# Channel mixing with seven block products, in an order planned at build time, and with re-arranged loads and stores

## The chip, the cores and the metric

One core of a Trainium2 chip runs the whole kernel. The metric is the device time of one execution in microseconds (us), and the median over executions is quoted. The profile is one execution taken by the hardware profiler; its span is 1 to 3 us shorter than the time of the same run. Engines are named as in the profile: PE is TensorE's matmuls, PEld its weight loads, DVE is VectorE, ACT ScalarE, POOL GpSimd, SP SyncE. Lines such as L807 are lines of the kernel in question. PSUM is the memory into which the matmuls write, used by the changed kernel as eight banks; SBUF holds the kernel's other tiles. A DMA transfer lands when its data have arrived. The granted clock is the share of TensorE's full clock that the profile shows. A run counts as slow when it is over 1.5% above the fastest of the same kernel.

A ratio below is formed from the fast runs of a kernel and of the kernel before in the same rounds, so it is not quite the ratio of the medians that stand beside it.

## The reference

```python
# q, k, v: (8, 8, 1024, 64); E, F: (64, 1024)
k_proj = einsum('ks,bhsd->bhkd', E, k); v_proj = einsum('ks,bhsd->bhkd', F, v)
attn   = softmax(q @ k_proj^T / 8) @ v_proj           # per batch and head
x      = attn as (8, 1024, 512)
u      = x + (relu(x^T @ w_tok1) @ w_tok2)^T          # token mixing
out    = u + relu(u @ w_ch1) @ w_ch2                  # channel mixing, 512 -> 1536 -> 512
```

Channel mixing is the largest part: three quarters of the old kernel's necessary matmul time.

## The kernel before

Batches run in a software pipeline: while channel mixing of batch b runs, the attention and token mixing ("front") of batch b+1 is dealt out between its blocks. The two channel products, for half a batch (512 tokens) at a time:

```python
def ch1(i, cc):                       # 12 times per half batch
    g_ps = psC.tile([P, S2], F32, ...)
    for dc in range(DMC):             # 4 matmuls of 512 columns
        nc.tensor.matmul(g_ps, wc1_sb[:, dc, cc*P:(cc+1)*P], uT[i][:, :, dc, :], ...)
    nc.scalar.activation(out=st["gT", i][:, cc, :], in_=g_ps, func=ACT.Relu)

def ch2(i, ss, part):                 # 4 rows x 3 parts per half batch
    for cc in range(part*4, part*4 + 4):
        nc.tensor.matmul(o2_ps, st["gT", i][:, cc, ss*P:(ss+1)*P], wc2_sb[:, cc, :], ...)
    if part == CC // 4 - 1:
        nc.vector.tensor_add(out=o_sb, in0=o2_ps, in1=u_sb[:, si, :])
        nc.sync.dma_start(out=out_v[b, :, si, :], in_=o_sb)
# ... (cut)
def q_transpose():                    # q of batches 1 to 7, by DMA, in SyncE's queue
    nc.sync.dma_start_transpose(out=qT[...], in_=q_sb[...])
```

The transposes of u (also DMA) and the stores of the output share SyncE's queue. Loads of k, v, q are double-buffered and issued from GpSimd's queue.

The softmax here doesn't subtract the row's maximum and nothing guards it: scores larger than these inputs give would overflow.

## Time and profile before

| what | value | where it is read |
|---|---|---|
| time | 502.83 us median of 3 (502.06 to 507.38) | timing runs |
| PE busy, whole span | 91% | page, part 1 |
| first channel product | 41.97 us | timeline of PE |
| stalls | mostly between 60 and 127 us | page, part 2; chain of waits |
| one batch in the steady state | 54.6 us | the same line returning in the chain |
| last matmul to the end | 3.9 us | timeline |

Part 1 of the page of the kernel before (busy us, share of the span, instructions), and rows of its part 2 (the span in 40 slices, tenths busy; PEclk is the granted TensorE clock):

```profile
PE 455.1 (91%) x2556; PEld 221.8 (44%) x2592; DVE 165.6 (33%) x304; ACT 167.3 (33%) x275; POOL 48.9 (10%) x72
...
PE   2689945975899999999999999999999999999996
...
PEclk9999995997899999999999999999999999999999
DMA  8999999999599249855592249505020411123102
```

From the twelfth slice on PE is 90% busy or more. In slices 6, 7, 9 and 10 it is 40 to 79% busy while the DMA engines are full, and the granted clock falls in slices 7, 10 and 11. The same in a table by windows (columns: window, its length, busy us of PE, PEld, DVE, ACT, POOL, granted clock, DMA share, GB/s):

```profile
60.00:80.00 20.00, 8.53 (x58) 3.26 (x55) 2.23 (x4) 6.72 (x12) 0.00 (x0) 0.83 1.22 192
...
150.00:200.00 50.00, 49.52 (x267) 23.46 (x271) 17.94 (x33) 19.06 (x32) 4.44 (x6) 1.00 0.64 132
```

The chain of the work that ended last, in order of time (start us, us, what):

```profile
51.68 29.44 DMA qT<-q_sb
...
106.90 20.44 DMA uT_698<-u_sb
...
173.85 1.73 PE o_ps L364 x8
...
228.43 1.73 PE o_ps L364 x8
...
283.01 1.73 PE o_ps L364 x8
```

Two DMA transposes take 29 and 20 us from issue to landing here, beside the loads; the median of q's transposes is 5.0 us, and those of u from 173 us on take 3.6 to 3.9. After them the chain is PE, and one of its lines comes back every 54.6 us. Two lines of PE's timeline say how fast matmuls go when nothing holds them back (start us, us until the last one ends, what, how many):

```profile
44.57 0.39 PE L286 MATMUL ut_ps<-ident,u_sb 128*128 128x128 bf16 x4
44.80 0.67 PE L276 MATMUL up_ps<-hT_sb,wt_sb 128*128 128x128 bf16 x8
```

From 44.57 to 44.80 PE starts four matmuls of 128 columns, each with its own weights: about 57 ns each. Matmuls of 512 columns start every 0.216 us. So in this trace the time follows the columns at these two sizes, and loading weights, a new set for every matmul, does not bind at either.

### The profile page before, as it was taken

What the parts mean: (1) busy time and instruction counts of PE and PEld (TensorE: products, weight loads), DVE (VectorE), ACT (ScalarE), POOL (GpSimd) and SP (SyncE); (2) the same over time, 40 slices, a digit from 0 to 9 for tenths busy, and PEclk for the clock granted to TensorE, in tenths of its full rate; (3) what the DMA queues carried; (4) which work ended last, traced back from release to release, by engine and by line L of the source; (5) the groups of instructions that cost most, each with busy time, mean ns of one, the idle gap of its engine ahead of it and who ended that gap; (6) DMA issues with size and microseconds to landing.
All of it is one profiled execution on the core that took longest, in us unless ns stands there. A gap on an engine that the chain in (4) does not pass through costs nothing.

```text
span 502.0 us, 6139 instructions
## 1 busy us (share of the span) xinstructions
PE 455.1 (91%) x2556; PEld 221.8 (44%) x2592; DVE 165.6 (33%) x304; ACT 167.3 (33%) x275; POOL 48.9 (10%) x72
## 2 busy tenths in 40 slices
PE   2689945975899999999999999999999999999996
PEld 1457412532345444544444444544444444444442
DVE  2354011533134332614242423533261424241102
ACT  1136641000453316150624135231615053423150
POOL 7533101301201002100200020000000000000000
PEclk9999995997899999999999999999999999999999
DMA  8999999999599249855592249505020411123102
GB/s 124 208 204 206 198 196 180 174 204 219 140 191 196 42 140 149 172 99 137 110 195 63 67 110 189 138 16 153 1 84 1 120 49 42 43 63 106 58 27 84
DMA packets 97211, 61.48 MB, mean 122 GB/s; under 512 B 60320, under 2 KB 88480, under 8 KB 97184
## 3 DMA queue, kind: packets, MB, share of 16 engines
q0 software_dynamic: 29728, 29.63, 36.5%
q1 hardware_dynamic: 67456, 31.46, 25.1%
q8 instruction: 20, 0.33, 0.2%
q14 instruction: 7, 0.06, 0.0%
HBM read 59.24 MB, written 16.78 MB: 151 GB/s over the span
## 4 chain that ended last, share of the span: by engine, by line
PE 73%; DMA 19%; ACT 3%; DVE 2%; POOL 1%; issue 1%; POOLq 0%
PE o_ps L364 31%; PE g_ps L353 26%; DMA qT<-q_sb 6%; PE h_ps L239 5%; PE u_ps L248 4%; DMA uT_698<-u_sb 4%; DMA q_sb<-in_q_dram 4%; DMA wc_sb<-in_moe_w_ch_dram 3%; PE o_ps L221 3%; PE kv_ps L174 2%; DMA v_sb<-in_v_dram 2%; PE s_ps L209 2%; ACT gT L357 1%; DMA out_dram<-o_sb 1%; DVE kp_sb L182 1%
## 5 line engine op out<-in xcount | busy, mean ns | idle before, releaser
L364 PE MATMUL o_ps<-wc_sb,gT 128*128 128x512 bf16 x738 | 183.3, 384 | 1.7 <-issue 0.2
L357 ACT ACTIVATE gT<-g_ps 128x512 bf16<-128x512 f32 x192 | 113.0, 600 | 213.7 <-PE g_ps L353 205.3
L353 PEld LDWEIGHTS <-wc_sb 128*128 128x128 bf16 x768 | 72.6, 98 | 91.8 <-issue 13.8
L364 PEld LDWEIGHTS <-gT 128*128 128x128 bf16 x768 | 73.5, 99 | 80.2 <-issue 4.8
L371 DVE TENSOR_TENSOR o_sb<-o_ps,u_sb 128x512 f32<-128x512 f32 x64 | 44.2, 691 | 90.1 <-PE o_ps L364 83.2
L252 DVE TENSOR_TENSOR u_sb<-u_ps,x_sb 128x512 bf16<-128x512 f32 x56 | 38.6, 690 | 87.7 <-PE u_ps L248 87.7
L214 ACT ACTIVATE a_sb<-s_ps 128x1024 bf16<-128x1024 f32 x32 | 32.1, 1033 | 41.8 <-PE s_ps L209 41.8
L229 DVE TENSOR_TENSOR x_sb<-o_ps,rdn 128x512 bf16<-128x512 f32 x64 | 44.2, 691 | 2.2
L248 PE MATMUL u_ps<-hT_sb,wt_sb 128*128 128x512 bf16 x112 | 34.1, 387 | 6.7 <-DVE u_sb L252 6.7
L228 DVE RECIPROCAL rdn<-o_ps 128x8 f32<-128x8 f32 x64 | 13.1, 204 | 64.8 <-PE o_ps L221 64.8
L221 PEld LDWEIGHTS <-a_sb 128*128 128x128 bf16 x256 | 20.8, 104 | 17.1 <-ACT a_sb L214 1.6
L78 POOL DMA_DIRECT2D k_sb<-in_k_dram x18 | 13.5, 751 | 143.6 <-PE kv_ps L177 136.3
L239 PE MATMUL h_ps<-x_sb,wt_sb 128*128 128x512 bf16 x106 | 26.1, 379 | 0.3
L182 DVE CAST kp_sb<-kv_ps 64x512 bf16<-64x512 f32 x8 | 5.5, 682 | 59.8 <-PE kv_ps L177 59.8
L209 PE MATMUL s_ps<-qT,kT 64*64 64x512 bf16 x128 | 12.8, 433 | 13.4 <-DMA qT<-q_sb 12.4
L248 PEld LDWEIGHTS <-wt_sb 128*128 128x128 bf16 x112 | 16.1, 144 | 19.3 <-issue 9.5
L86 POOL DMA_DIRECT2D q_sb<-in_q_dram x18 | 13.3, 741 | 92.8 <-DMA qT<-q_sb 85.4
L177 PE MATMUL kv_ps<-v_sb,FT_sb 128*64 128x512 bf16 (+1 forms) x88 | 17.4, 354 | 5.3 <-DMA v_sb<-in_v_dram 5.3
L174 PE MATMUL kv_ps<-k_sb,ET_sb 128*64 128x512 bf16 (+1 forms) x88 | 18.3, 355 | 2.0 <-DMA k_sb<-in_k_dram 2.0
L239 PEld LDWEIGHTS <-wt_sb 128*128 128x128 bf16 x112 | 10.9, 98 | 13.3 <-issue 0.2
L243 ACT ACTIVATE hT_sb<-h_ps 128x512 bf16<-128x512 f32 x14 | 8.4, 597 | 25.2 <-PE h_ps L239 25.2
L353 PE MATMUL g_ps<-uT_698,wc_sb 128*128 128x512 bf16 x48 | 12.9, 422 | 3.6 <-DMA uT_698<-u_sb 3.6
(67 smaller groups left out, 325.2 us busy)
## 6 DMA issues: line engine op xcount, KB each, us to landing
out_dram<-o_sb SPq DMA_DIRECT2D x64, 256.0 KB, 2.1
k_sb<-in_k_dram POOLq DMA_DIRECT2D x14, 512.0 KB, 9.7
v_sb<-in_v_dram POOLq DMA_DIRECT2D x14, 512.0 KB, 11.5
q_sb<-in_q_dram POOLq DMA_DIRECT2D x14, 512.0 KB, 10.0
wc_sb<-in_moe_w_ch_dram POOLq DMA_DIRECT2D x8, 384.0 KB, 17.4
k_sb<-in_k_dram POOLq DMA_DIRECT2D x4, 256.0 KB, 7.4
v_sb<-in_v_dram POOLq DMA_DIRECT2D x4, 256.0 KB, 8.0
q_sb<-in_q_dram POOLq DMA_DIRECT2D x4, 256.0 KB, 10.0
```

Of the source, the lines that this page charges most:

```text
L174: nc.tensor.matmul(kv_ps[0:KP, hs], ET_sb[:, si, :], k_sb[:, hs, si, :], start=a, stop=z)
L209: nc.tensor.matmul(s_ps[dst * KP : (dst + 1) * KP, h % 2, :], kT[rows, h, :], qT[rows, h].rearrange("p j s -> p (j s)"), start=True, stop= ...
L214: nc.scalar.activation(out=a_sb, in_=s_ps, func=ACT.Exp, scale=scale)
L221: nc.tensor.matmul(o_ps[:, j // 2, (j % 2) * 2 * D1 : (j % 2 + 1) * 2 * D1], a_sb[:, h % 2, j * P : (j + 1) * P], vb[:, h // 2, h % 2].rea ...
L229: nc.vector.tensor_tensor(out=x_sb[:, :, h * D : (h + 1) * D].rearrange("p (n c) d -> p n c d", n=2), in0=o4[:, :, :, 0:D], in1=rdn[:, :, ...
L239: nc.tensor.matmul(h_ps, wt1_sb[:, si, t * P : (t + 1) * P], x_sb[:, si, :], start=(si == 0), stop=(si == NSI - 1),)
L248: nc.tensor.matmul(u_ps, wt2_sb[:, t, si::NSI], hT_sb[:, t, :], start=(t == 0), stop=(t == TC - 1),)
L252: nc.vector.tensor_add(out=u_sb[:, si, :], in0=u_ps, in1=x_sb[:, si, :])
L353: nc.tensor.matmul(g_ps, wc1_sb[:, dc, cc * P : (cc + 1) * P], uT[i][:, :, dc, :], start=(dc == 0), stop=(dc == DMC - 1),)
L357: nc.scalar.activation(out=st["gT", i][:, cc, :], in_=g_ps, func=ACT.Relu)
L364: nc.tensor.matmul(o2_ps, st["gT", i][:, cc, ss * P : (ss + 1) * P], wc2_sb[:, cc, :], start=(cc == 0), stop=(cc == CC - 1),)
L371: nc.vector.tensor_add(out=o_sb, in0=o2_ps, in1=u_sb[:, si, :])
```

## The change

The intent is to do channel mixing with fewer matmul columns. Each of the two products is cut into 2 by 2 blocks (halves of the tokens, of the inner and of the outer dimension), and seven block products with sums and differences of blocks replace the eight ordinary ones. Half a batch then needs 168 matmuls of 256 columns in place of 96 of 512: seven eighths. The price is additions: combined weights once, four bf16 sums of u per half batch, partial products kept by ScalarE, saturating additions with a relu on VectorE, and, at the output, ScalarE copies to which GpSimd adds u.

Because PE then waits on many small steps, the order of all engines is fixed at build time by a planner: a list scheduler that knows an assumed duration of every step and the eight PSUM banks. The diff at its core (cuts marked):

```diff
-        def ch1(i, cc): ...
-        def ch2(i, ss, part): ...
+    def up_set(j, m):                      # 3 sets per half batch
+        bk = {n: Bank("U", seeded=n == "y") for n in "xyz"}
+        product(1)                                              # 4 matmuls of 256 columns into x
+        act(512, lambda: nc.scalar.copy(out=view("y"), in_=view("x")), ...)   # seeds bank y
+        product(2); relu(0, "x"); product(6); keep(ub, "ub")
+        product(7); product(5); keep(ua, "ua")
+        dve(512, lambda: add_relu(G[:, 2, cs], view("z"), ua), ...)
+        product(3); relu(1, "y"); product(4)
+        dve(512, lambda: add_relu(g21, view("z"), ub), ...)
+        total(3, ...); total(5, ...); total(4, ...); total(6, ...)            # bf16, SBUF only
+    def s_sums(j):                         # four bf16 sums of blocks of uT, on VectorE
+    def down_block(j):                     # seven products again, 12 matmuls each
+        def copy_add(dst, key, src, sh, dh):                    # three times per half batch
+            act(512, lambda: nc.scalar.copy(out=dst, in_=view(src)), ...)
+            pool(512, lambda: nc.gpsimd.tensor_add(out=dst, in0=dst, in1=u_of(sh, dh)), ...)
+        # ... (cut)
+        queue = nc.gpsimd if j < NSB - 1 else nc.sync           # stores
+class Planner:                             # orders every engine's work, picks PSUM banks
+    def dve(cols, fn, ps=True, **kw):      # the durations it assumes
+        t = cols / 960 + 0.07 if ps else cols / 1920 + 0.07
+        return pl.add("DVE", t, t + 0.09, fn, **kw)
+    def act(cols, fn, **kw):
+        t = cols / 1200 + 0.07
+        return pl.add("ACT", t, t + 0.105, fn, **kw)
+    # ... (cut)
+            if b == 1:                     # q of batch 1 is transposed on TensorE
+                for hp in range(2 * i, 2 * i + 2):
+                    unit(0.4, lambda t, hp=hp: q_transpose_pe(hp, t))
+    # ... (cut)
+    def tie(j, other):                     # loads and DMA transposes take turns
+        j.deps.add(other)
+        tied[j] = other
+    # ... (cut)
+            for _ in range(int((j.start - idle - 0.3) / 0.216) if spare is not None else 0):
+                blank(spare)               # filler matmuls on zeros while the first loads come in
```

The durations in the diff are what the program assumes.

Batch 0 and the weights are loaded head pair by head pair (k, v, q of a pair together); k, v and q have one buffer instead of two. Matmuls accumulate onto a bank that ScalarE has filled; eight matmuls on zeros, one per bank, come first. With them the results are correct.

## The prediction

> What bounds the kernel now. From about 127 us on, TensorE. The chain of waits that ended last is 73% PE, and the same line returns in it every 54.58 us (173.85, 228.43, 283.01): the steady time of one batch. In the windows from 150 to 450 us PE is 99% busy at granted clock 1.00; VectorE and ScalarE are each 33% busy over the span. Before 127 us the bound is DMA: the chain runs over the wc and q loads, a qT transpose (51.68 to 81.1 us) and a uT transpose (20.44 us), and the windows from 60 to 100 us show PE half idle or worse, clock 0.83. Some 35 us go there. The first channel product starts at 41.97 us.
>
> Removed. Channel mixing is 1536 matmuls of 512 columns; the timeline paces 16 in 3.45 us, 0.2157 each, 331 us. The new order has 2688 of 256 columns, estimated at 0.109 us from that pace, 293 us: 38 us fewer, all on the critical path, unless weight loads bind. The timeline says not: four transposes of 128 columns, each with its own weights, take 0.22 us, 56 ns each.[...] The rest of PE's work (attention, token mixing, transposes) at the trace's paces is 106 us: 399 us of necessary PE time (437 in the old).
>
> Added. Per batch VectorE gets 12 saturating adds from PSUM (0.61 us back to back, like the 512-column additions here), 32 bf16 additions without PSUM[...] and narrower attention tiles: about 37 us of a 49 us batch. ScalarE: some 50 tiles of 512[...], 27 us. Neither binds on average; bursts will cost PE small gaps. GpSimd gets 6 additions a batch.[...] these additions have slack.
>
> Moved. Q of batch 1 is transposed on PE, and transposes and loads take turns, so the two long transposes should become 4 to 5 us ones. Attention of batch 0 starts per head pair as loads land: first channel product near 35 us. Stores move behind GpSimd's waits, and with single buffers for q, k, v the loads depend on that queue's order: 0 to 2 us of stall a batch.
>
> Sum: 399 us PE work + 20 us lost to the first loads + 5 us around batch 1 + 8 us of bubbles (2%) + 6 us tail (last addition, a 512 KB store) = 438 us, range 424 to 456. Chances: faster by over 2% 0.97, within 2% 0.02, slower 0.01.
>
> Right, if the profile shows: up and down products at 109 ns pace; batch period 49 to 50.5 us; PE over 95% busy at clock 1.00 from about 60 us; VectorE 70 to 80% busy, ScalarE 50 to 60%; no transpose landing above 8 us; a chain mostly PE. Wrong, if: 256-column matmuls pace well above 109 ns; PE waits for ScalarE's PSUM-to-PSUM copies or the saturating adds; PE waits for a transpose held back by a load in GpSimd's queue; the clock drops in such gaps; the start is no shorter than 42 us.
>
> What would make it wrong: the planned order is static, so a latency that the plan underrates repeats in every block; a period of 52 us would give about 458 us.

Two assumed durations are terms that the trace of before does not show, that of a bf16 addition on VectorE and that of a tile of 512 on ScalarE. The sums that they went into came to 37 and 27 us a batch and stay as estimates. The trace of before agrees with the 27: one such tile takes ScalarE 0.60 us and two in a row 1.08, so 50 take 27 to 30 us (an estimate from these two). It has no bf16 addition without PSUM to support the 37; the trace of the changed kernel has 0.42 us for one.

## The result, and the profile after

The changed kernel takes 441.2 us (440.64 to 442.14, 4 runs) against 505.11 (502.06 to 511.97) in the same comparison: ratio 0.8808, 95% interval 0.8743 to 0.8873, all of its runs fast. (The medians listed here give 0.873.)

Parts 1 and 2 of the page of the changed kernel:

```profile
PE 417.0 (95%) x3726; PEld 336.1 (77%) x3754; DVE 323.8 (74%) x782; ACT 242.2 (55%) x440; POOL 124.7 (28%) x152
...
PE   7899999999999999999999899999999999999993
...
PEclk9999999999999999999999999999999999999998
DMA  9999999569799786978339894397830403151122
```

The hole in slices 6 to 10 is gone, at PE and in the clock. VectorE's share has more than doubled. The windows that answer to those of before, and a wide one over the steady state:

```profile
60.00:80.00 20.00, 19.72 (x177) 15.59 (x175) 13.95 (x44) 11.35 (x20) 5.59 (x6) 1.00 1.18 217
...
150.00:200.00 50.00, 48.68 (x420) 39.22 (x423) 41.16 (x95) 27.12 (x51) 14.56 (x18) 1.00 0.84 163
```

```profile
100.00:350.00 250.00, 242.75 (x2095) 195.36 (x2112) 198.73 (x472) 140.06 (x254) 62.32 (x72) 1.00 0.76 146
```

From 100 to 350 us PE is idle for 7.25 us. Two lines of its timeline give the pace of the new products, and two more, the start of a batch's token mixing, give the period:

```profile
97.05 0.60 PE L807 MATMUL ps<-S,wT 128*128 128x256 bf16 x4
97.49 0.60 PE L807 MATMUL ps<-S,wc_sb 128*128 128x256 bf16 x4
...
154.04 1.04 PE L617 MATMUL ps<-x_sb,wt_sb 128*128 128x512 bf16 x3
...
204.91 1.03 PE L617 MATMUL ps<-x_sb,wt_sb 128*128 128x512 bf16 x3
```

Four matmuls of 256 columns start within 0.44 us: 0.109 us each, as predicted. The period here is 50.9 us (45.6 before it, then 50.7, 50.5 and 48.9), against 54.6.

Where PE's 7 us go is seen in the longest of its waits in the steady state, in the timeline of all engines (in brackets: idle time before the instruction, and what ended it):

```profile
247.96 1.51 POOL L324 DMA_DIRECT2D q_sb<-in_q_dram  x2 [10.11 <-issue]
...
248.65 3.40 DVE L677 TENSOR_TENSOR S<-uT 128x512 bf16<-128x512 bf16 x1
...
249.47 1.18 POOL L936 TENSOR_TENSOR db<-db,u 128x512 f32<-128x512 f32 x1
...
250.59 1.16 POOL L936 TENSOR_TENSOR o<-o,u 128x512 f32<-128x512 f32 x1
251.97 0.68 DVE L788 CUSTOM_DVE_ANT_0 G<-ps,ua 128x512 bf16<-128x512 f32 x1
...
252.70 0.60 PE L807 MATMUL ps<-uT,wT 128*128 128x256 bf16 x4 [2.37 <-DVE G L788]
```

A bf16 sum on VectorE that takes 0.42 us elsewhere takes 3.40, and ends 0.3 us after two GpSimd additions have ended. The saturating addition behind it is late, and PE waits 2.37 us for that. Over the whole trace VectorE runs 276 additions whose two inputs and output are bf16 in SBUF. Those that no GpSimd addition overlaps take 0.42 us (0.55 for the wider weights). Of 33 that one does overlap, 15 take more than 0.6 us, 13.8 us beyond 0.42 in all. Additions that read PSUM are not longer under such an overlap (0.69 us at most). It goes the other way too: from 90.02 us on a GpSimd addition takes 2.22 us in place of about 1.15, while three bf16 sums of VectorE run through at 0.41. One thing stays open: the sum of 3.40 us is late from 248.65 us on, 0.8 us before the first GpSimd addition begins by the record, while GpSimd issues a load; yet 69 such sums overlap a DMA issue of GpSimd alone, and none of these takes over 0.43 us.

So two questions stood open. How much of the 64 us do the seven products bring, and how much the order and the loads? And do the GpSimd additions, which cost PE nothing by the sum of busy times, cost the kernel time?

**Theory 1**: the smaller column count pays 38 us in the steady state, the order and the loads pay some 25 us, once, in the first 130 us. **Its rival**: most comes from the order and the loads. **Theory 2**: GpSimd's additions hold back VectorE's SBUF additions and through them PE. **Its rival**: slack absorbs it.

### The profile page after: what moved, and what is told of

Its sections match the earlier page's. It is cut to its first block, busy times and chain, and to the rows that moved or that the text cites. A ratio compares the mean times of both kernels' runs of the same rounds, so it can differ in the third digit from the quotient of the medians.

```text
span 438.8 us, 9331 instructions
## 1 busy us (share of the span) xinstructions
PE 417.0 (95%) x3726; PEld 336.1 (77%) x3754; DVE 323.8 (74%) x782; ACT 242.2 (55%) x440; POOL 124.7 (28%) x152
## 4 chain that ended last, share of the span: by engine, by line
PE 74%; DVE 12%; DMA 9%; ACT 2%; issue 1%; POOL 0%; DVEq 0%; ACTq 0%
PE ps L902 27%; PE ps L807 25%; DMA v_sb<-in_v_dram 6%; PE ps L617 5%; PE ps L637 5%; DVE S L677 3%; PE ps L465 3%; DMA uT<-u 3%; PE ps L586 2%; DVE G L842 2%; PE ps L563 2%; PE ps L387 2%; DVE x_sb L603 2%; DVE g L788 1%; DVE u L648 1%
## 5 line engine op out<-in xcount | busy, mean ns | idle before, releaser
L902 PEld LDWEIGHTS <-G 128*128 128x128 bf16 x1344 | 130.2, 98 | 26.6 <-issue 4.4
L902 PE MATMUL ps<-wc_sb,G 128*128 128x256 bf16 x768 | 104.1, 273 | 2.4 <-DVE da L952 1.6
L829 ACT ACTIVATE G<-ps 128x512 bf16<-128x512 f32 x96 | 57.4, 600 | 58.5 <-PE ps L807 58.3
L902 PE MATMUL ps<-wT,G 128*128 128x256 bf16 x576 | 78.2, 273 | 1.0 <-DVE o L956 1.0
L807 PEld LDWEIGHTS <-wT 128*128 128x128 bf16 x576 | 55.2, 98 | 15.3 <-issue 4.3
L807 PE MATMUL ps<-S,wc_sb 128*128 128x256 bf16 x384 | 57.6, 273 | 0.3
L807 PE MATMUL ps<-uT,wc_sb 128*128 128x256 bf16 x384 | 57.6, 273 | 0.1
L807 PE MATMUL ps<-S,wT 128*128 128x256 bf16 x384 | 55.6, 273 | 0.2 <-DVE S L677 0.2
L603 DVE TENSOR_TENSOR x_sb<-ps,rdn 128x256 bf16<-128x256 f32 x128 | 50.4, 416 | 0.5
L842 DVE TENSOR_TENSOR G<-G 128x512 bf16<-128x512 bf16 x96 | 45.4, 476 | 3.4 <-DVE G L842 0.5
L934 ACT COPY o<-ps 128x512 f32<-128x512 f32 x32 | 18.8, 587 | 21.6 <-PE ps L902 21.3
## 6 DMA issues: line engine op xcount, KB each, us to landing
v_sb<-in_v_dram POOLq DMA_DIRECT2D x14, 512.0 KB, 11.9
```

The lines of the kernel that those rows point to most:

```text
L603: lambda: nc.vector.tensor_tensor(out=x_sb[:, 4 * half : 4 * half + 4, h * D : (h + 1) * D], in0=view()[:, :, 0:D], in1=rdn[:, :, None].to ...
L807: nc.tensor.matmul(t[:, c, :], w1_of(n, dd, 2 * m + c), a_of(j, n, dd), start=(n in (1, 7) and c == 0 and dd == 0), stop=(c == 1 and dd == 1),
L829: lambda: nc.scalar.activation(out=G[:, n, cs], in_=view(src), func=ACT.Relu),
L842: 512, lambda: f(out=G[:, n, cs], in0=in0, in1=in1), ps=False, reads=deps,
L902: nc.tensor.matmul(view(X_OF[n])[:, t, :], G[:, G_OF[n], cc, t * P : (t + 1) * P], w2_of(n, cc), start=(n in (1, 7) and t == 0 and cc == 0 ...
```

## The experiments

Twelve experiments ran, the last with the unaltered changed kernel. All gave correct results but one. A variant that changes jobs or dependencies is planned anew, so its order differs as a whole; where only one queue was changed and the orders of PE, VectorE and ScalarE are the same, this is said.

### 1. The new order with the ordinary eight products

```diff
-            s_sums(j)
-            for m in range(SETS): up_set(j, m)
+            for n in range(CC): up_chunk(j, n)   # 4 matmuls of 512 columns, one relu
-            down_block(j)                         # seven products, copies, GpSimd additions
+            down_block(j)                         # 4 rows of 12 matmuls, one VectorE addition each
-    TU = 24.65
+    TU = 27.3                                     # the planner's time per half batch
# ... (cut: other due times in the plan move with it)
```

> The changed kernel's planner, loads, stores and attention, but ordinary channel mixing: 1536 matmuls of 512 columns, no sums, no combined weights, one relu per product and one addition per output row block. Theory 1 (the smaller count of product columns pays in the steady state, and the schedule pays mainly in the first 130 us): the batch period returns to 54 to 55 us, the first channel product still starts at 30 to 33 us, total 465 to 480 us, that is about 30 to 35 us over the changed kernel and 25 to 35 us under the kernel before. Rival (most of the 64 us comes from the planned order and the loads): total below 455 us.

Measured: 465.17 us (464.87 to 465.45), ratio 0.9234. In the same rounds the kernel before took 504.47. Token mixing of batches 4 and 5 begins here (timeline of PE):

```profile
211.26 1.03 PE L586 MATMUL ps<-x_sb,wt_sb 128*128 128x512 bf16 x4
...
265.55 1.03 PE L586 MATMUL ps<-x_sb,wt_sb 128*128 128x512 bf16 x4
```

The period is 54.3 us, almost that of the kernel before, so in the steady state the new order gives the old products nothing. Yet the kernel is 39 us faster. That comes once, at the start: by the gaps between the starts of matmuls (which also hold a few missing records), PE stands still for about 50 us between its first matmul and 127 us in the kernel before, and for about 11 us here (filler matmuls count as work). The seven products then add 24 us (465.17 to 441.2), not 38. The interval of 465 to 480 that theory 1 named just holds the result; its shares do not. The truth lies between the theories, nearer to the rival: about 39 us by order and loads, 24 by the products. The first channel product starts at 34.92 us here, later than the 30 to 33 that was expected, and 31.38 in the changed kernel; the plan is a new one, so the 24 us are not strictly the products' alone.

### 2. The kernel before, with q of batch 1 transposed on TensorE

```diff
-        units = [kv_proj, lambda: (k_transpose(), q_transpose())]
+        units = [kv_proj, k_transpose] + [lambda hp=hp: q_transpose_pe(hp) for hp in range(HP)]
```

> The kernel before, with one edit: q of batch 1 is transposed on TensorE (32 transposes, 4 VectorE copies) instead of by two DMA transposes. Theory 1 (the 29 us landing of those DMA transposes, among the loads, is what stalls TensorE between 60 and 82 us): the stall of about 25 us in the scores of batch 1 goes, and 10 to 22 us of the total with it: 480 to 493 us. Rival (the loads themselves are late, and the next wait, for the uT transpose at 107 us, takes the time over): 497 us or more.

Measured: 500.64 us median of 4 (492.80 to 504.45). Three of the runs are over 1.5% above the fastest and so count as slow. By the medians, slow runs included, the edit gains 4 us on the kernel before (504.47 in the same rounds), by the fastest runs 9 (492.80 against 501.37), and the one fast run is 11 us below the mean of the five fast ones of the kernel before (503.88): the size stays open. The profiled run is one of those called slow, at a mean clock of 0.978, as in the profile of the kernel before (0.976). It shows two waits of PE in its timeline:

```profile
110.59 1.01 PE L248 MATMUL u_ps<-hT_sb,wt_sb 128*128 128x512 bf16 x2 [7.15 <-DVE u_sb L252]
...
122.77 6.34 PE L353 MATMUL g_ps<-uT,wc_sb 128*128 128x512 bf16 x16 [5.27 <-DMA uT<-u_sb]
```

The first stall is gone: from 60 to 82 us PE is busy for 21.86 us, against 9.36 in the kernel before. From 82 to 128 us it is busy for 27.75, against 35.30. Token mixing of batch 1 begins 13.4 us earlier (82.5 against 95.9 us), that of batch 2 only 3.6 us earlier (155.7 against 159.3). Between them PE waits for VectorE, VectorE waits 13.3 us for stores to free its output tiles, and the stores stand in SyncE's queue behind q transposes of batches 2 and 3, which hold the queue for 19 and 8 us. So at least in this run most of the stall was handed on rather than removed, as the rival has it; that one late transpose was not the whole cause is as much as this experiment says.

### 3. The changed kernel with q of batch 1 transposed by DMA

```diff
-            if b == 1:
-                for hp in range(2 * i, 2 * i + 2):
-                    unit(0.4, lambda t, hp=hp: q_transpose_pe(hp, t))
...
-            if b > 0:
-                q_transpose(b + 1)
+            q_transpose(b + 1)      # for batch 1 without a load of its own and without a turn
```

> The changed kernel with q of batch 1 transposed by two DMA transposes, planned anew. Theory 1: they land among the loads of batch 1 and take over 15 us each instead of the 5 us of later ones, TensorE stalls in the front of batch 1, total 450 to 462 us. Rival (planning gives enough slack for it): within 3 us of the changed kernel, 438 to 445 us.

Measured: 462.36 us (457.70 to 465.73; the run of 465.73 counts as slow, and the three fast ones have a mean of 460.81), ratio 0.9148. The longest wait of PE in total (what waited for what: us, times, longest us), and the times to landing of the transposes of q:

```profile
PE ps L564 <- DMA qT<-q_sb: 18.8, 2, 12.7
```

The two waits in PE's timeline:

```profile
68.17 1.01 PE L564 MATMUL ps<-qT,kT 128*128 128x512 bf16 x2 [6.09 <-DMA qT<-q_sb]
...
151.91 0.58 PE L564 MATMUL ps<-qT,kT 128*128 128x512 bf16 x1 [12.66 <-DMA qT<-q_sb]
```

```profile
DMA to landing us min/median/max: 4.4/5.9/18.1
```

The cost is about 20 us in fast runs, at the upper end of the forecast, and PE waits 18.8 us for transposes of q. But the theory explains only a third of that. The transposes of batch 1 are issued at 50.0 and 58.9 us and land after 18.1 and 17.1 us, and PE's wait for them is the first one, 6.1 us. The longer wait, 12.7 us, is for q of batch 3: its transpose is issued at 134.9 us, beside loads of k and v issued from 133.2 us on, and lands after 16.9 us. So the new plan has a second collision later on, and the 20 us are not the price of batch 1 alone. In the changed kernel no transpose of q lands later than 8.4 us. The same edit was worth 4 to 11 us in the kernel before; how much of the difference is due to the new plan was not tried.

### 4. The changed kernel without turns between loads and transposes

```diff
     def tie(j, other):
-        j.deps.add(other)
-        tied[j] = other
+        pass
```

> The changed kernel without the rule that loads and transposes take turns (the extra dependencies are not made; data dependencies stay), planned anew. Theory 1: transposes now overlap loads and land in 8 to 20 us instead of 4.8, and TensorE waits for some of them: 446 to 460 us. Rival (from batch 2 on the DMA engines have room, the turns are not needed): within 3 us, or faster because loads start earlier.

Measured: 463.87 us (462.19 to 466.38), ratio 0.9213, a cost of 22.7 us and more than was expected.

```profile
PE ps L806 <- DMA uT<-u: 11.9, 1, 11.9
PE ps L585 <- DVE x_sb L602: 9.5, 6, 2.4
```

```profile
DMA to landing us min/median/max: 4.3/5.9/17.3
```

The second fence is again the landing of the transposes of q. One transpose of u makes PE wait 11.9 us; the rest is spread over many waits, and the period of the later batches is about 52 instead of 50.7 us. As the order was planned anew, not all of the 22.7 us can be put down to the transposes.

### 5. Stores in SyncE's queue

```diff
-        queue = nc.gpsimd if j < NSB - 1 else nc.sync
+        queue = nc.sync
```

> The changed kernel with every store issued from SyncE's queue instead of GpSimd's; the orders on TensorE, VectorE and ScalarE are the same as in the changed kernel. Theory 1: stores then sit in one queue with the transposes; a transpose waits behind a store whose output is not ready, or the store's packets lengthen it; total 1 to 8 us longer. Rival: the queue of the stores does not matter: within 1.5 us. A third: it is faster by 1 to 3 us because GpSimd is relieved of 30 issues of 0.57 us and its loads leave earlier.

The orders on PE, VectorE and ScalarE are identical. Measured: 456.17 us median of six (453.04 to 456.41 in the five fast runs, their median 456.09), ratio 0.9113: a cost of about 15 us, twice the most that was expected. A sixth run, the one that was profiled, took 728.01 us at a mean granted clock of 0.563:

```profile
PEclk8555555555555555555555555555555555555555
```

It is one of 6 runs and no other variant showed it. From 200 to 400 us PE was busy all the time at a clock of 0.56; why the clock was so low is not known, and that profile cannot show where the 15 us of the fast runs go. That the stores' queue matters is shown; that transposes wait behind stores whose data are not ready is only argued.

### 6. GpSimd's additions shrunk to one element (wrong)

```diff
-    nc.gpsimd.tensor_add(out=dst, in0=dst, in1=u_of(sh, dh))
+    nc.gpsimd.tensor_add(out=dst[:, 0:1, 0:1], in0=dst[:, 0:1, 0:1], in1=u_of(sh, dh)[:, 0:1, 0:1])
```

> Wrong result on purpose: the 48 GpSimd additions of 512 elements shrink to one element each, the orders on all other engines are the same. In the changed kernel's trace the bf16 VectorE additions last 0.418 us, except 32 that overlap a GpSimd addition: those last until it ends (up to 3.4 us), about 14 us in all; TensorE then waits 2.37, 0.82 and 0.68 us behind them. Theory 2 (GpSimd additions hold VectorE's two-SBUF-input additions back, and it reaches TensorE): no such addition lasts over 0.45 us, the sum of VectorE's busy time falls by about 14 us, total 2 to 7 us shorter, 434 to 439 us. Rival (slack absorbs it): within 1 us of the changed kernel.

Measured: 432.69 us (431.91 to 433.95), ratio 0.8665, 8.5 us less than the changed kernel, where 2 to 7 were expected; the result is wrong. (The expectation speaks of 32 long additions; in the trace 33 overlap, one of them by 12 ns, and 15 are long.) The steady window, and the group of bf16 sums of G, here and then in the changed kernel (the group's busy us and mean ns come after the bar):

```profile
100.00:350.00 250.00, 249.90 (x2177) 201.03 (x2175) 194.68 (x492) 143.49 (x261) 36.49 (x73) 1.00 0.76 145
```

```profile
L842 DVE TENSOR_TENSOR G<-G 128x512 bf16<-128x512 bf16 x96 | 39.8, 417 | 3.4 <-DVE G L842 0.5
```

```profile
L842 DVE TENSOR_TENSOR G<-G 128x512 bf16<-128x512 bf16 x96 | 45.4, 476 | 3.4 <-DVE G L842 0.5
```

PE's idle time from 100 to 350 us falls from 7.25 to 0.10 us. The smaller additions also leave GpSimd's queue freer for loads, which is a rival; but of the waits of PE that the changed kernel's trace lists in this window (6.3 us in all) 5.4 us were ended by VectorE and only 0.9 by a load. Here none is left. So in the steady state practically all of PE's remaining idle time came from GpSimd's additions, although GpSimd was idle for 72% of the time and VectorE for 26%. Theory 2 holds, its rival falls.

### 7. GpSimd's additions done twice

```diff
                 nc.gpsimd.tensor_add(out=dst, in0=dst, in1=u_of(sh, dh)),
+                nc.gpsimd.tensor_add(out=spare_t, in0=spare_t, in1=u_of(sh, dh)),
```

> The dose in the other direction: after each of the 48 GpSimd additions a second one of the same size into a spare tile; orders on the other engines the same. Theory 2: the long VectorE additions double in number (about 28 us extra in all), batch period grows by 0.5 to 1 us, total 3 to 9 us longer, 444 to 450 us. Rival: within 1 us of the changed kernel, as GpSimd is idle 70% of the time.

The orders on the other engines are the same, but for one memset of the spare tile on VectorE. Measured: 462.64 us (461.62 to 463.71), ratio 0.9259. The cost of 21 us is more than double what was expected. The sums of u (in the view of one tile: duration in ns, shortest, median, longest), first in the changed kernel, then here:

```profile
L677 DVE TENSOR_TENSOR S<-uT x32: 394/418/3402, 34.9 to 392.4; 128x512 bf16<-128x512 bf16 x32
```

```profile
L679 DVE TENSOR_TENSOR S<-uT x32: 392/416/5606, 35.8 to 414.4; 128x512 bf16<-128x512 bf16 x32
```

The median is untouched, the longest grows to 5.6 us. All such bf16 additions over 0.6 us are 32 now, 34.4 us beyond 0.42, where the changed kernel has 15 and 13.8 us. The dose goes the right way, but GpSimd's loads and stores stand behind the additional work as well, so not all 21 us need be VectorE's.

### 8. A plan that takes evictions for free

```diff
     def dve(cols, fn, ps=True, **kw):
-        t = cols / 960 + 0.07 if ps else cols / 1920 + 0.07
-        return pl.add("DVE", t, t + 0.09, fn, **kw)
+        return pl.add("DVE", 0.02, 0.02, fn, **kw)      # likewise ScalarE and GpSimd
```

> The same instructions, but the planner is told that every VectorE, ScalarE and GpSimd step takes 0.02 us, so that it orders TensorE's work as if results left PSUM at once. Theory 1 (the order that knows the eviction times is what keeps TensorE 95% busy although VectorE is 74% busy): TensorE waits for ScalarE's copies and VectorE's sums in every block, total 465 us or more. Rival (any order with enough PSUM banks does): within 6 us of the changed kernel's 441.

Measured: 531.06 us (530.38 to 532.89), ratio 1.0623: 90 us over the changed kernel and slower than the kernel before.

```profile
PE 439.5 (83%) x3707; PEld 344.2 (65%) x3741; DVE 332.7 (63%) x782; ACT 244.5 (46%) x440; POOL 122.4 (23%) x152
```

```profile
PE ps L899 <- DVE da L949: 20.9, 14, 5.2
```

The period is 57.8 us, although the same matmuls run. PE waits for VectorE's first output addition 14 times, up to 5.2 us, and for many others less. The start suffers too (first channel product at 47.2 us, clock 0.65 in the first 31 us, with 13 filler matmuls fewer). With this plan the kernel with seven products is slower than the one before: its gain depends on an order that knows how long PSUM takes to empty. The eight ordinary products were not planned in this way, so what the wrong durations would cost them is not known.

### 9. No filler matmuls

```diff
-            for _ in range(int((j.start - idle - 0.3) / 0.216) if spare is not None else 0):
-                blank(spare)
```

> The changed kernel without the filler matmuls on zeros in TensorE's waits of the first 30 us (the eight that touch each bank once stay). Theory 1: they hold the granted clock at 1.00 while the loads come in; without them the clock of the first 30 us falls below 0.9 and the first channel product starts 1 to 4 us later, total 442 to 446 us. Rival: the loads set the start, and it makes no difference (within 1 us).

Measured: 444.72 us (444.37 to 445.28), ratio 0.8900. The row of the clock:

```profile
PEclk9799999999999999999999989999999999999999
```

The clock falls to 0.91 in the first 12 us and 0.88 from 12 to 31, where the changed kernel has 1.00 in both. But the first channel product starts at 31.97 us, only 0.6 us later, so the 3 us are not explained by a late start, and the expected mechanism is not shown. The time goes in later batches, one of which has a period of 53.1 us. A second profile of the unaltered changed kernel (experiment 12) has a batch of 52.2 us in the same place, where the first has 50.7. Its window from 252 to 256 us, then that of the first profile:

```profile
252.00:256.00 4.00, 3.37 (x19) 2.50 (x19) 3.83 (x11) 0.00 (x0) 0.00 (x0) 0.60 1.02 168
```

```profile
252.00:256.00 4.00, 3.28 (x29) 2.72 (x30) 4.00 (x14) 1.07 (x2) 0.00 (x0) 1.00 1.05 174
```

All three profiles have a PE wait of 2.4 to 2.6 us for a late saturating addition just before this place. In two of them, this experiment's and experiment 12's, the granted clock then drops to 0.50 for 3.4 us (in experiment 12 to 0.60 over the window of 4 us above), which by itself is about 1.7 us of full-speed work (an estimate, half of 3.4); in the first profile it does not. Why it drops in one and not in the other is open. So in two of the three profiles more was lost at this place than the wait itself, and fillers or not is not what decides this batch.

### 10. The additions on VectorE, straight from PSUM

```diff
-            act(512, lambda: nc.scalar.copy(out=dst, in_=view(src)), ...)
-            pool(512, lambda: nc.gpsimd.tensor_add(out=dst, in0=dst, in1=u_of(sh, dh)), ...)
+            dve(512, lambda: nc.vector.tensor_add(out=dst, in0=view(src), in1=u_of(sh, dh)), ...)
```

> A version meant to be better: the 48 pairs of ScalarE copy and GpSimd addition become 48 VectorE additions straight from PSUM, planned anew; GpSimd then only issues DMAs. Theory 2 (GpSimd's additions block VectorE): no bf16 addition over 0.45 us; VectorE gains 48 times 0.61 to 0.69 us and loses 14 us of blocked time, about 78 to 80% busy; total 433 to 438 us, most of the 8.5 us that the one-element version gained. Rival (VectorE is the next bound, and 33 us more on it costs as much as the blocking): 439 us or more.

Measured: 433.64 us median; three fast runs of 432.13 to 433.81 and a slow one of 439.37, which was the profiled one. Its clock is 0.996, so the clock does not explain it; PE waits 5.4 us in it for a transpose of q that landed after 22.1 us. Ratio of the fast runs 0.8659. Moving 48 additions onto VectorE, the busiest engine after PE, made the kernel faster: what they cost there is less than what they cost from GpSimd. Part of the gain may come from the new plan or from the 48 copies that ScalarE is spared; this was not taken apart.

### 11 and 12. That version with shorter last stores, and the changed kernel once more beside it

```diff
+            if j == NSB - 1:                 # last block: four stores of 256 KB, each when ready
+                for dh in (0, 1) if sh == 0 else (1, 0): ... nc.sync.dma_start(out=out_v[b, :, rows, cols], ...)
```

> The version with the additions on VectorE, and with the last block's two 512 KB stores cut into four of 256 KB, each issued when its own half is ready; the order of all other work is the same. Expected: the end comes 0.5 to 1.5 us after the last TensorE work sooner than with whole stores, total 431 to 434 us in fast runs; against the changed kernel on the same chip 1.5 to 2.2% shorter. Rival (the one fast-looking median of the additions on VectorE was luck of chip or state): within 1% of the changed kernel.

> The changed kernel, unaltered, on the chip of the run beside it: 440.5 to 442.5 us, as when it was first timed. It is the yardstick for the version with additions on VectorE and a short tail.

Measured, on one chip and in the same rounds: 433.69 us (432.47 to 437.12, ratio 0.8680) and 441.90 us (440.61 to 447.52; the run of 447.52 counts as slow; ratio 0.8827). The version with additions on VectorE is 1.9% faster by the medians (1.7% by the two ratios). The six runs of the one (437.12 at most) lie below all of the other (at least 440.61), so it beats both kernels, though by less than 2%. Its page, and its steady window:

```profile
PE 417.8 (96%) x3725; PEld 337.1 (78%) x3754; DVE 338.5 (78%) x830; ACT 218.4 (50%) x392; POOL 66.3 (15%) x104
```

```profile
100.00:350.00 250.00, 246.78 (x2129) 199.35 (x2147) 206.22 (x506) 129.37 (x230) 29.42 (x44) 0.99 0.76 145
```

VectorE's busy time grows by only 15 us for 48 additions of 0.69, since 13.8 us of blocked time go away, and additions that follow each other start every 0.61 us. The shorter stores gave nothing: from the last matmul's end to the end of the span it is 4.5 us with them and 4.5 without. PE still waits once, 2.2 us, for a transpose of q that landed after 19 us, so this version is not the end of it either.

## Why the prediction was right, and where it was not

The time was predicted at 438 us with a range of 424 to 456; it is 441.2. Several terms behind the sum were off and cancelled, so that 438 came this close is in part luck.

- **Pace of the products: right.** 0.109 us per matmul of 256 columns, as estimated; weight loads do not bind. At 128 columns with new weights for each matmul, both traces show 55 to 62 ns at a granted clock of 1.00.
- **"38 us fewer, all on the critical path": the columns are right, their worth was not.** With planned order and the same loads the seven products bring 24 us (experiment 1). Of the 14 us given back, GpSimd's additions account for 8.5 (experiment 6), 1.0 of it at the end (5.6 us from the last matmul to the end, 4.6 in experiment 6). Some 5 us are not assigned to anything.
- **The moved work was put too low.** The prediction gave the start and batch 1 no total of their own, but 65 us were forecast in all (502.83 less 438), and less 38 that leaves about 27. Experiment 1 shows 39 us for the order and the loads.
- **"20 us lost to the first loads": too much.** By gaps between starts of matmuls, PE lost 9 us before its first channel product, besides 2.9 us before its very first matmul; that product started at 31.4 us rather than 35. Part of the rest is filler work, which does not count as a gap. From there to 127 us PE is idle for 3.3 us, where 5 were put down around batch 1.
- **"8 us of bubbles": the size about right, the cause not named.** From 100 to 350 us it was 7.25 us alone, and the periods were 48.9 to 50.9 us after a first one of 45.6, for 49 to 50.5 given. The prediction mentioned that GpSimd and VectorE might get in each other's way and set it aside because "these additions have slack". That sentence failed. GpSimd's additions do have slack (it is 28% busy); those of VectorE that they hold back (up to 3.40 us in place of 0.42) do not. So one of the prediction's own signs of being wrong did show: PE waited for a saturating addition (3.1 us in two waits), and in the profile of experiment 12 the clock dropped after such a wait (0.60 over 4 us). It was small enough to stay inside the range.
- **Loads of the engines: right.** VectorE 74% (70 to 80 predicted), ScalarE 55% (50 to 60). "No transpose landing above 8 us": the longest took 8.4.
- **"The planned order is static": right, and stronger than was thought.** It was put as a risk of some 20 us; a plan with all its evictions near zero costs 90 us (experiment 8).

The parts do not add up. Taking one away makes a new plan, or lets another transfer collide: the q transposes on PE are worth about 20 us in the changed kernel (a third of it at batch 1) and 4 to 11 in the kernel before, the turns 23, the stores' queue 15.

## What to carry to other kernels

An algebraic saving on the busiest engine is worth its full size only if the work that it adds elsewhere never makes that engine wait (here 24 of 38 us were left): measure the saving with the order held fixed, and read the single longest waits rather than the busy shares. An engine that is idle most of the time can still be the wrong place for a step, if it blocks an engine that is on the chain (here GpSimd, idle for 72% of the time, cost 8.5 us); shrinking the step to one element tells at once about what it costs. When a late transfer stalls the start, look for the next transfer that will collide before counting the gain (in experiment 3 PE waited 6.1 us for the first and 12.7 for the next).
